# Second token block on the weight operands left from the first, third block's operand sums on VectorE, u sums next to u

## The chip, the cores and the metric

The kernel runs on one core of a Trainium2 chip. The metric is the device time of one execution in microseconds. TensorE (PE) multiplies into PSUM; VectorE (DVE), ScalarE (ACT) and GpSimd (POOL) work on rows of 128 partitions; SyncE (SP) issues the transfers here. Each engine works through its own instructions in order, and semaphores tie the engines together.

## The reference, cut to what matters

Attention over 4 x 8 heads of 576 tokens gives x, 2,304 tokens by 512; then comes a gated feed-forward layer:

```
x = attention(q, k, v, M_prev, z_prev, beta)      # (2304, 512)
g = x @ w_gate                                    # (512, 1536)
silu = g * (1.0 / (1.0 + np.exp(-g)))
val = x @ w_val                                   # (512, 1536)
out = (silu * val) @ w_out                        # (1536, 512)
```

Below, u is silu * val. The change touches the feed-forward layer alone.

## The kernel before, in words

Every product of fp32 numbers is made of three matmuls in fp32r: each operand is split into a high and a low part (a ScalarE cast, a VectorE subtraction), and high x high, high x low and low x high are summed in PSUM.

**Attention** runs over 16 pairs of heads and writes x, in a high and a low part, to the DRAM tensors `xdh` and `xdl`.

**Feed-forward, first product.** The tokens are cut into three blocks of 768 (`ORDER`), the 1,536 features into `NF` = 12 blocks f of 128. A step f takes 128 columns of `w_gate` and of `w_val`. For f = 0 to 2 of block 1 it is a plain product (`eight`). Everywhere else it is a Winograd form of 2 x 2 blocks with seven products instead of eight: `operands(f)` makes the weight side out of the weights `wr[f]` (sums `t`, and high and low parts `th`, `tl`, `bh`, `bl`, two buffers each, which successive f's take in turn), `sums` and the loads of `direct` make the x side (the fourteen tiles `xs` for the block at hand; `x3` for block 3). `chain` gives the seven steps p1, p2, p6, p7, p5, p4, p3, of six matmuls each; step n writes one of two PSUM banks in turn (`ring`), and after most steps ScalarE or VectorE reads that bank. `seven` runs one chain; `plan[n]` holds other work that is issued after step n.

The order on PE, ACT, DVE and POOL is program order (`queued`). The transfers on SP are placed by the scheduler.

- **Block 1, f = 0 to 11.** Its u is split at once, and `lower`, with f one step behind, multiplies it by `w_out`, into six PSUM banks `po`. Beside it the weights of each f arrive in three thirds (`third`), are decoded, kept in DRAM (`wdr`, `wdw`), and the third of `w_out` is split and its two parts stored to `wdo` (in `low_part`). The x side of block 2 is made in f = 6 to 11 (`sums(ORDER[1])`: the loads begin before f = 6, an add of high and low part in plan 5 of each of the next f's).
- **Block 2, f = 0**, alone, with the last `lower` of block 1, and `away`, which takes `po` to the output.
- **Block 3, f = 0**, alone. `sums_on_pool` loads block 3's x from `xdh` and `xdl` and makes its sums and splits on GpSimd.
- **Blocks 2 and 3, f = 1 to 11**, two chains step by step in turn. `stored` makes u (`weighed`) and stores it to `udr`. `tees` makes the four differences of `w_out`'s quarters (`combine` on GpSimd), splits them, and stores both parts to `tdr`.
- **The w_out stage** for blocks 2 and 3: again seven products, in 42 chunks (seven products, two blocks, three chunks `c` of two feature pairs), 18 matmuls of 128x256 in each. `raw_in` loads u's quarters, GpSimd makes one of the sums (six instructions), VectorE the others (`s3`, `s2`, `s4`: 18), `prep` splits a chunk's u, `tee` loads the `w_out` side already split, and `taken` and `out_to` bring the results out.

A double f means one f of blocks 2 and 3 together: 84 matmuls; a single f of one block is 42.

Of the kernel before, what the change touches and what calls it, by code (L numbers as in the profile page):

```python
# [9 lines left out]
F32 = mybir.dt.float32  # L10
# [35 lines left out]
def attention_moe(ctx: ExitStack, tc: tile.TileContext, qt, kt_, v, m, beta, wg, wv, wo, out):  # L46
# [13 lines left out]
    wdo = dram.tile([NF, 128, 2, 512], F32, name="wdo")  # L60
    wdw = dram.tile([NF, 128, 512], F32, name="wdw")
    tdr = dram.tile([4, 2, 128, NF // 2, 256], F32, name="tdr")
    udr = dram.tile([2, 2, 2, 128, NF // 2, N2], F32, name="udr")
# [640 lines left out]
    tmp = tc.alloc_tile_pool(name="tmp", bufs=1, side="right", reuse_waits="tile")  # L704

# [52 lines left out]
    def sums(t0, here=False):  # L758

        got = rot(tmp, "xr", [128, 4, 2, N2], F32, 1)  # L760
        a21, a22, a11, a12 = (got[:, n] for n in range(4))
        s1, s = (rot(tmp, name, [128, 2, N2], F32, 1) for name in ("xt", "xm"))
# [24 lines left out]
    def sums_on_pool(xs, t0, pool_):  # L787

        got = pool_.tile([128, 4, 2, N2], F32, name="xr3")
        s1, s = (pool_.tile([128, 2, N2], F32, name=name) for name in ("xt3", "xm3"))  # L790
        two = (s, s1)
        a21, a22, a11, a12 = (got[:, n] for n in range(4))

        def load(n):
            for dst, src in ((got[:, n], xdh), (two[n % 2], xdl)):
                SP.dma_start(dst, block(src, t0, *AT[n]))  # L796

        load(0)
        load(1)
        for n in range(4):  # L800
            pool.tensor_tensor(got[:, n], got[:, n], two[n % 2], op=ALU.add)
            if n + 2 < 4:
                load(n + 2)
        for p, i, j in (("p1", 0, 0), ("p2", 0, 1), ("p4", 1, 1)):
            direct(xs, t0, p, i, j)

        def parts(p, x):
            h, l = xs[p]
            split_hi(h, x)
            pool.tensor_tensor(l, x, h.bitcast(F32), op=ALU.subtract)  # L810

        pool.tensor_tensor(s1, a21, a22, op=ALU.add)
        pool.tensor_tensor(s, s1, a11, op=ALU.subtract)
        parts("p6", s)
        pool.tensor_tensor(a11, a11, a21, op=ALU.subtract)
        parts("p7", a11)
        parts("p5", s1)
        pool.tensor_tensor(a12, a12, s, op=ALU.subtract)
        parts("p3", a12)

    def high(mix, p, k):
# [29 lines left out]
    def away(j):  # L851
        pt = rot(tmp, "pt", [128, 512], F32, 6)
# [54 lines left out]
    def chain(w, x, bank, use):  # L907
# [28 lines left out]
    def seven(w, x, bank, use, down, plan, away_at):  # L936
        step = chain(w, x, bank, use)
# [10 lines left out]

    def stored(b, f):
# [12 lines left out]
    for f in range(NF):  # L962
        plain, left = f < PLAIN, NF - 1 - f
        plan = [[] for _ in range(4 if plain else 7)]
        if left < 2:
            again(1 - left)
# [3 lines left out]
        if f + 1 >= PLAIN:  # L970
            ready[f + 1], work = operands((f + 1) % NF)
# [68 lines left out]
    tmp.release()  # L1040

    def tees(r, tp):
        w2 = rot(tp, "w2", [128, 2, 512], F32, 2)
        tq = rot(tp, "tq", [128, 4, 256], F32, 1)
        parts = [rot(tp, f"tq{part}", [128, 4, 256], F32R, 2) for part in "hl"]
# [8 lines left out]
        def tops_():  # L1054
            act.copy(parts[0], tq)

        def rest():
            dve.tensor_tensor(parts[1], tq, parts[0].bitcast(F32), op=ALU.subtract)
            for n, x in enumerate(parts):
                SP.dma_start(tdr[:, n, :, r, :].rearrange("i p c -> p i c"), x.bitcast(F32))  # L1060

        return combine, tops_, rest
# [4 lines left out]
    uraw, tset = {}, {}  # L1067
    QUARTER = dict(p1=(0, 0), p2=(0, 1), p6=(0, 0), p7=(1, 0), p4=(1, 0), p5=(1, 1), p3=(0, 1))
    split_in = [xs[p] for p in STEPS] + [x3[p] for p in STEPS]
    ops = {}  # L1070

    def raw_in(p_, b, q, c, of=None):
        if (b, q, c) not in uraw:
            uraw[b, q, c] = p_.tile([128, 2, N2], F32, name=f"u{b}{q[0]}{q[1]}{c}")
        i, j = of or q
        SP.dma_start(uraw[b, q, c], udr[b, i, j, :, 2 * c : 2 * c + 2])

    def prep(n):
        if n >= len(chunks):
            return  # L1080
        k, b, c = chunks[n]
        src = uraw[b, QUARTER[k], c]
        ops[n] = h, l = split_in[n % len(split_in)]
        act.copy(h, src)
        dve.tensor_tensor(l, src, h.bitcast(F32), op=ALU.subtract)
        if k == "p7":
            raw_in(None, b, (1, 0), c, (1, 1))

    wdo_ = wdo.rearrange("(r j) p h c -> j h p r c", j=2)
# [188 lines left out]
```

## Time and profile before

| | us |
|---|---|
| median of 3 runs (lowest to highest) | 642.76 (642.56 to 644.46) |
| the profiled execution | 643.69 |
| its span, first to last instruction | 641.9 |
| busy: PE / DVE / ACT / POOL | 597.7 / 469.9 / 387.5 / 276.9 |
| mean granted TensorE clock over the span | 0.960 |

All rows are from the one profiled execution. Its own time is 1.8 us longer than its span and 0.9 us longer than the median of the runs. The granted clock is 1.00 at 2.4 GHz and 0.50 at 1.2 GHz. A busy TensorE is not one at its peak: its busy time counts slower matmuls at the lower clock as well.

### The profile page before, as it was taken

The numbers are of one execution on the slowest core, as the hardware profiler recorded it, in microseconds if no ns is written. First come the engines' busy times: TensorE is split into PE (matmuls) and PEld (weight loads), VectorE is DVE, ScalarE is ACT, GpSimd is POOL, SyncE is SP. The second block draws the span as 40 slices with busy tenths as digits, with TensorE's granted clock in tenths as the row PEclk, the third lists the DMA queues.
The fourth block names the chain that finished last, engine by engine and source line by source line (L and its number), as shares of the span: only waits on it lengthen the run. The fifth ranks groups of instructions, "written<-read, shape, count | busy, mean of one in ns | idle before, by whom it ended". The sixth has DMA issues, their size and how long they took to land.

```text
span 641.9 us, 11934 instructions
## 1 busy us (share of the span) xinstructions
PE 597.7 (93%) x4118; PEld 549.5 (86%) x4118; DVE 469.9 (73%) x1118; ACT 387.5 (60%) x884; POOL 276.9 (43%) x307
## 2 busy tenths in 40 slices
PE   6999999999999999999972399999999999888997
PEld 4888888878889999999962299999999999778997
DVE  6899999999989888899960045777666556498770
ACT  8889898988876777767550144555555445126711
POOL 6999999999743343344003940223300000530000
PEclk9999999999999999999995589999999999789999
DMA  8366665856276587984759043665559224944642
GB/s 241 124 183 209 198 230 171 261 166 212 91 276 217 189 285 246 383 299 172 253 167 350 16 140 104 204 202 199 180 177 348 82 98 149 383 182 156 238 149 74
DMA packets 69020, 128.45 MB, mean 200 GB/s; under 512 B 8160, under 2 KB 37984, under 8 KB 68960
## 3 DMA queue, kind: packets, MB, share of 16 engines
q1 hardware_dynamic: 68672, 127.41, 59.3%
q8 instruction: 32, 0.52, 0.4%
q10 hardware_dynamic: 288, 0.30, 0.2%
q14 instruction: 28, 0.23, 0.1%
HBM read 82.06 MB, written 45.61 MB: 199 GB/s over the span
## 4 chain that ended last, share of the span: by engine, by line
PE 82%; DMA 6%; POOL 4%; DVE 4%; ACT 2%; issue 1%; SPq 1%; ACTq 0%; POOLq 0%; DVEq 0%
PE s L89 54%; PE tr L89 28%; DMA u<-udr 2%; DVE u L89 2%; DMA xm<-xdl 1%; DMA xr<-xdh 1%; POOL xr L89 1%; DMA qr<-in_qt_dram 1%; DVE yp5l L89 0%; SPq L796 0%; POOL ps L89 0%; DVE oc L89 0%; DMA udr<-zg 0%; DVE yp7l L89 0%; POOL yp3l L89 0%
## 5 line engine op out<-in xcount | busy, mean ns | idle before, releaser
L89 DVE TENSOR_TENSOR zv<-s,zv 128x384 f32<-128x384 f32 x33 | 18.4, 557 | 56.4 <-PE s L89 54.8
L89 POOL TENSOR_SCALAR we<-we 128x512 f32<-128x512 f32 x32 | 25.6, 802 | 74.4 <-ACT we L89 74.3
L89 POOL TENSOR_SCALAR pl<-pl,rs,og 128x384 f32<-128x384 f32 (+1 forms) x64 | 54.0, 855 | 5.0 <-DVE rs L89 4.5
L89 POOL TENSOR_TENSOR u<-u,u 128x768 f32<-128x768 f32 x6 | 14.5, 2438 | 87.4 <-DMA u<-udr 87.3
L89 PE MATMUL tr<-g,vp 128*64 128x320 f32 (+4 forms) x448 | 48.8, 360 | 0.2 <-ACT g L89 0.2
L89 ACT ACTIVATE zh<-zh 128x384 f32<-128x384 f32 x33 | 17.4, 526 | 49.0 <-DVE zh L89 49.0
L89 DVE TENSOR_TENSOR zg<-s,zp 128x384 f32<-128x384 f32 x33 | 18.3, 556 | 38.5 <-PE s L89 21.6
L89 ACT ACTIVATE pl<-pl,mx 128x384 f32<-128x384 f32 (+1 forms) x64 | 42.4, 664 | 4.2 <-DVE mx L89 3.6
L89 PEld LDWEIGHTS tr<-g,vp 128*64 128x64 f32 x448 | 29.3, 137 | 18.1 <-issue 2.3
L89 POOL TENSOR_TENSOR tq<-w 128x256 f32<-128x256 f32 x12 | 10.2, 869 | 71.2 <-DVE tql L89 71.2
L89 PE MATMUL s<-kh,qh 64*128 64x128 f32 (+4 forms) x160 | 36.1, 378 | 4.3 <-POOL qh L89 4.1
L89 ACT COPY zp<-s 128x384 f32<-128x384 f32 x33 | 15.7, 476 | 39.7 <-PE s L89 39.3
L89 DVE CUSTOM_DVE_ANT_0 pl<-s,maskp 128x384 f32<-128x384 f32 (+1 forms) x64 | 38.3, 618 | 0.7 <-PE s L89 0.3
L89 ACT COPY g<-tr 128x384 f32<-128x384 f32 (+1 forms) x60 | 29.9, 524 | 4.7 <-PE tr L89 4.6
L89 POOL TENSOR_SCALAR ps<-ps,rs,og 128x128 f32<-128x128 f32 (+1 forms) x64 | 31.8, 508 | 1.4 <-DVE rs L89 1.4
L89 ACT ACTIVATE ps<-ps,mx 128x128 f32<-128x128 f32 (+1 forms) x64 | 28.6, 454 | 6.1 <-DVE mx L89 6.0
L89 PE MATMUL s<-kl,qh 64*128 64x128 f32 (+4 forms) x160 | 31.1, 325 | 0.9 <-POOL kl L89 0.9
L89 PE MATMUL s<-kh,ql 64*128 64x128 f32 (+4 forms) x160 | 31.1, 325 | 0.0
L89 DVE COPY g<-tr 128x384 f32<-128x384 f32 (+2 forms) x60 | 29.8, 515 | 1.5 <-PE tr L89 1.4
L89 DVE TENSOR_TENSOR tl<-tt,th 128x512 fp32r<-128x512 f32 x42 | 30.5, 727 | 0.0
L89 PE MATMUL tr<-ident,pl 128*128 128x128 f32 x210 | 29.8, 281 | 0.1
L89 DVE TENSOR_TENSOR u<-u,u 128x768 f32<-128x768 f32 x18 | 21.7, 1225 | 10.1 <-POOL u L89 10.1
(483 smaller groups left out, 2332.7 us busy)
## 6 DMA issues: line engine op xcount, KB each, us to landing
u<-udr SPq DMA_DIRECT2D x30, 384.0 KB, 8.6
wraw<-in_wg_dram SPq DMA_DIRECT2D x12, 512.0 KB, 4.4
wraw<-in_wv_dram SPq DMA_DIRECT2D x12, 512.0 KB, 5.1
wraw<-in_wo_dram SPq DMA_DIRECT2D x12, 512.0 KB, 5.0
wr<-wdr SPq DMA_DIRECT2D x12, 512.0 KB, 4.4
qr<-in_qt_dram SPq DMA_DIRECT2D x15, 384.0 KB, 3.1
vp<-in_v_dram SPq DMA_DIRECT2D x16, 320.0 KB, 5.2
xdh<-xh SPq DMA_DIRECT2D x16, 288.0 KB, 4.2
```

The lines of the kernel that those rows point to most:

```text
L89: ins = getattr(eng, name)(*args, **kw)
```

## The change

1. **Order of f.** Block 2 begins with f = 11 and 10 (`LATE`), whose weight operands are still in the two buffers; block 3 follows with f = 10 and 11; then come the double f's, 0 to 9. The operands of f = 0 are made in block 3's f = 11 and no longer in block 1's f = 11.
2. **Block 3's sums.** `sums` takes a pool and a name, and makes block 3's raw sums on VectorE as well: the loads begin at the end of block 1's f = 10 (`begin3`), three adds are in f = 11, the fourth and the four Winograd sums in block 2's f = 11. ScalarE and VectorE split them in block 2's f = 10. `sums_on_pool` goes.
3. **Sums of u.** `mixed` makes the four Winograd sums of u's quarters on VectorE from the tiles in which u was made (128x384), and stores the results; `udr` has a DRAM tensor for each product and block. They run one at a time in the gaps (`some_sums`); the last eight run in the first four chunks of the w_out stage.
4. **w_out in fp32.** `wdo` goes, `tdr` holds unsplit differences, and `split_t` splits the `w_out` side on chip in the w_out stage. Each chunk's u has a load of its own (`load_u`, six ahead), `LEAD` is 3 instead of 5.
5. **Buffers.** `hold` has two buffers of each kind (one of `zv`) in block 1; `pt` has four instead of six; blocks 2 and 3 get their own in the pool `z2`.

```diff
-            if j == 2:
-                for i, o in enumerate((oh, ol)):
-                    SP.dma_start(wdo[f, :, i], o.bitcast(F32))
...
-    def sums(t0, here=False):
-        got = rot(tmp, "xr", [128, 4, 2, N2], F32, 1)
+    def sums(t0, pool_, name, here=False):
+        got = rot(pool_, f"{name}r", [128, 4, 2, N2], F32, 1)
...
-    def sums_on_pool(xs, t0, pool_):
...
-    HOLD = dict(zp=3, zg=4, zh=4, zv=2)
-    hold = lambda name: rot(zwp, name, [128, N2], F32, HOLD[name])
+    hold = lambda name: rot(zwp, name, [128, N2], F32, 1 if name == "zv" else 2)
...
     def stored(b, f):
         def use(i, g, v):
             weighed(g, v)
-            SP.dma_start(udr[b, i, f % 2, :, f // 2], g)
+            kept_u[b, f, i] = g
+            if (f % 2, i) != (0, 1):
+                keep(b, {(0, 0): "p1", (1, 0): "p2", (1, 1): "p4"}[f % 2, i], f, g)
+            if i and (b, f ^ 1, 0) in kept_u:
+                sums_due.extend(mixed(b, f))
         return use
+
+    def mixed(b, f):
+        a11, a21, a12, a22 = (kept_u.pop((b, f // 2 * 2 + j, i)) for j in range(2) for i in range(2))
+        s3, s2 = (rot(z2p, f"zs{n}{b}", [128, N2], F32, 1) for n in range(2))
+        s4 = a11 if f % 2 else a12
+        def one(k, out, x, y, op):
+            def run():
+                dve.tensor_tensor(out, x, y, op=op)
+                keep(b, k, f, out)
+            return run
+        return [
+            one("p7", s3, a11, a21, ALU.subtract), one("p5", a21, a21, a22, ALU.add),
+            one("p6", s2, a22, s3, ALU.subtract), one("p3", s4, a12, s2, ALU.subtract),
+        ]
...
-        if f + 1 >= PLAIN:
-            ready[f + 1], work = operands((f + 1) % NF)
+        if NF > f + 1 >= PLAIN:
+            ready[f + 1], work = operands(f + 1)
...
         if left == 1:
             for k, work in zip((1, 3, 5), due[4:]):
                 plan[k].append(work)
+            begin3, due3, mix3 = sums(ORDER[2], xr3p, "y")
+            plan[6].append(begin3)
         if left == 0:
+            for k, work in zip((0, 1, 5), due3):
+                plan[k].append(work)
...
+    LATE = NF - 1, NF - 2
     plan = [[] for _ in range(7)]
-    again(2)
-    w0 = ready.pop(NF)
-    w1, work = operands(1)
-    for k, some_ in [*enumerate(work), *arrive]:
+    for k, some_ in arrive:
         plan[k] += some_
+    for k, i in ((0, 3), (1, 4), (3, 5), (5, 7), (6, 6)):
+        plan[k].append(due3[i])
-    seven(w0, xs, ring2, stored(0, 0), down, plan, (3, 5, 6))
+    seven(ready[LATE[0]], xs, ring2, stored(0, LATE[0]), down, plan, (3, 5, 6))
...
-    with tc.tile_pool(name="xr3", bufs=1, reuse_waits="tile") as xr3p:
-        sums_on_pool(x3, ORDER[2], xr3p)
-    seven(w0, x3, ring3, stored(1, 0), [], [[] for _ in range(7)], (0, 2, 4))
+    for p, i, j in (("p1", 0, 0), ("p2", 0, 1), ("p4", 1, 1)):
+        direct(x3, ORDER[2], p, i, j)
+    plan = [[] for _ in range(7)]
+    for k, p in ((0, "p6"), (1, "p7"), (2, "p5"), (4, "p3")):
+        plan[k].append(high(mix3, p, both, x3))
+    for k, p in ((1, "p6"), (2, "p7"), (3, "p5"), (6, "p3")):
+        plan[k].append(low(mix3, p, both, x3))
+    seven(ready[LATE[1]], xs, ring2, stored(0, LATE[1]), [], plan, (0, 2, 4), holds(0))
...
+    again(1)
+    w1, work = operands(0)
+    for k in (0, 1, 2, 4):
+        plan[k].append(some_sums)
+    seven(ready[LATE[1]], x3, ring3, stored(1, LATE[1]), [], plan, (0, 2, 4), holds(1))
...
+    plan[0].append(tees(0))
+    seven(ready[LATE[0]], x3, ring3, stored(1, LATE[0]), [], plan, (), holds(1))
...
+    def load_u(n):
+        if n < len(chunks):
+            k, b, c = chunks[n]
+            raw_u[n] = rot(p3a, "ur", [128, 2, N2], F32, U_AHEAD)
+            SP.dma_start(raw_u[n], udr[b, k][:, 2 * c : 2 * c + 2])
...
+    def split_t(n, c):
+        if n < len(KS):
+            k = KS[n]
+            if c == 0:
+                tset[k] = [rot(p3b if n % 2 else p3a, f"t{n % 2}{part}", [128, NF // 2, 256], F32R, 1) for part in "hl"]
+            rows = slice(2 * c, 2 * c + 2)
+            h, l = (x[:, rows] for x in tset[k])
+            act.copy(h, raw_t[k][:, rows])
+            dve.tensor_tensor(l, raw_t[k][:, rows], h.bitcast(F32), op=ALU.subtract)
+            if c == NC - 1:
+                load_t(n + 2)
...
-    for b in range(2):
-        for c in range(NC):
-            s1 = uraw[b, (1, 1), c]
-            pool.tensor_tensor(s1, s1, uraw[b, (1, 0), c], op=ALU.add)
...
-        for s, *which in sums_at.get(n + LEAD, ()):
-            s(*which)
+        at = n // 6
+        if n % 6 in (1, 2, 4):
+            split_t(at + 1, (1, 2, 4).index(n % 6))
+        some_sums(2)
         prep(n + LEAD)
```

In the double f's the plan holds `some_sums` at steps 1, 5, 7 and 9 of 14, `split_t(0, c)` and the first three `prep` in f = 9.

## Rows read from the trace of the kernel before

**Rows 1.** Table by stages (start:end, length, busy us of each engine, granted clock, DMA).
```profile
309.68:321.24 11.56, 11.56 (x61) 10.79 (x61) 10.78 (x22) 7.46 (x17) 0.00 (x0) 1.00 0.86 285
321.24:332.60 11.36, 11.36 (x60) 10.45 (x59) 9.71 (x20) 8.50 (x18) 0.00 (x0) 1.00 0.35 104
332.60:374.65 42.05, 15.47 (x43) 11.91 (x43) 2.25 (x5) 3.99 (x8) 25.89 (x18) 0.55 0.59 204
374.65:535.32 160.67, 160.67 (x925) 160.67 (x925) 101.11 (x188) 80.60 (x161) 19.51 (x23) 1.00 0.50 165
535.32:585.15 49.83, 42.03 (x309) 40.28 (x308) 36.18 (x36) 13.94 (x20) 14.47 (x6) 0.90 0.66 238
585.15:638.49 53.34, 53.33 (x448) 53.12 (x448) 30.82 (x38) 22.11 (x34) 0.00 (x0) 1.00 0.50 171
```
The engines' columns are PE, PEld, DVE, ACT and POOL, with instructions in brackets.

**Rows 2.** Waits of TensorE from 326 to 382 us (total, times, longest).
```profile
PE s L89 <- DMA yp1h<-xdh: 12.6, 1, 12.6
PE s L89 <- POOL yp6h L89: 9.5, 1, 9.5
```

**Rows 3.** Timeline of GpSimd in block 3's f = 0 (start, us).
```profile
355.24 1.80 POOL L89 TENSOR_TENSOR xt<-xr 128x768 f32<-128x768 f32 x1
```

**Rows 4.** Timeline of GpSimd and VectorE at the w_out stage's start.
```profile
553.10 14.58 POOL L89 TENSOR_TENSOR u<-u,u 128x768 f32<-128x768 f32 x6 [87.32 <-DMA u<-udr]
563.40 5.10 DVE L89 TENSOR_TENSOR u<-u,u 128x768 f32<-128x768 f32 x2
```

**Rows 5.** Timeline of VectorE in block 1's f = 11.
```profile
309.75 0.54 DVE L89 SCALAR_TENSOR_TENSOR zg<-s,zg 128x384 f32<-128x384 f32 x1
310.21 0.54 DVE L89 SCALAR_TENSOR_TENSOR zh<-zv,zh 128x384 f32<-128x384 f32 x1
...
311.89 0.56 DVE L89 TENSOR_TENSOR zg<-s,zp 128x384 f32<-128x384 f32 x1
...
314.50 0.95 DVE L89 TENSOR_TENSOR xr<-xr 128x768 f32<-128x768 f32 x1
```

**Rows 6.** Chain that ended last: first and last of eight pieces.
```profile
587.24 6.46 PE tr L89 x54
...
632.00 6.49 PE s L89 x54
```

**Rows 7.** Timeline of TensorE and VectorE at the end of block 2's f = 0.
```profile
331.95 0.39 PE L89 MATMUL tr<-woh,uh 128*128 128x512 f32 x1
...
332.15 0.56 DVE L89 SCALAR_TENSOR_TENSOR zg<-s,zg 128x384 f32<-128x384 f32 x1 [0.54 <-PE s L89]
```

**Rows 8.** Timeline of ScalarE at two places.
```profile
331.95 0.59 ACT L89 ACTIVATE pt<-tr 128x512 f32<-128x512 f32 x1
...
535.18 0.83 ACT L89 CAST xp5h<-u 128x768 fp32r<-128x768 f32 x1
535.91 0.83 ACT L89 CAST xp4h<-u 128x768 fp32r<-128x768 f32 x1
```

**Rows 9.** DMA issues of the whole span (count, KB each, median us to landing).
```profile
u<-udr SPq DMA_DIRECT2D x30, 384.0 KB, 8.6
...
xm<-xdl SPq DMA_DIRECT2D x4, 384.0 KB, 5.4
...
xp1l<-xdl SPq DMA_DIRECT2D x2, 384.0 KB, 3.6
```

**Rows 10.** Timeline of SyncE in block 1's f = 11.
```profile
310.60 0.37 SPq L754 DMA_DIRECT2D xp1l<-xdl  x1
```

**Rows 11.** Table of 2 us slices of the w_out stage, columns as in rows 1.
```profile
548.00:550.00 2.00, 0.32 (x1) 0.11 (x1) 0.00 (x0) 0.87 (x2) 0.00 (x0) 1.00 1.04 375
550.00:552.00 2.00, 1.04 (x5) 1.04 (x6) 0.00 (x0) 0.00 (x0) 0.00 (x0) 0.50 1.03 410
...
556.00:558.00 2.00, 2.00 (x16) 2.00 (x15) 2.00 (x1) 0.00 (x0) 2.00 (x2) 0.80 1.02 393
...
580.00:582.00 2.00, 1.54 (x13) 1.34 (x12) 1.91 (x4) 0.39 (x1) 0.00 (x0) 1.00 0.00 0
```

More of the change, by code (lines that the diff above doesn't have):

```diff
@@ L59, in attention_moe @@
     wdr = dram.tile([NF, 128, 1024], F32, name="wdr")
-    wdo = dram.tile([NF, 128, 2, 512], F32, name="wdo")
     wdw = dram.tile([NF, 128, 512], F32, name="wdw")
-    tdr = dram.tile([4, 2, 128, NF // 2, 256], F32, name="tdr")
-    udr = dram.tile([2, 2, 2, 128, NF // 2, N2], F32, name="udr")
+    tdr = dram.tile([4, 128, NF // 2, 256], F32, name="tdr")
+    udr = {(b, k): dram.tile([128, NF // 2, N2], F32, name=f"u{k}{b}") for k in STEPS for b in range(2)}
     slots = {}
@@ L704, in attention_moe @@
     tmp = tc.alloc_tile_pool(name="tmp", bufs=1, side="right", reuse_waits="tile")
+    xr3p = tc.alloc_tile_pool(name="xr3", bufs=1, side="right", reuse_waits="tile")
     def again(f):
@@ L785, in sums, with high, low @@
         return lambda: (load(0), load(1)), work, mix
-    def sums_on_pool(xs, t0, pool_):
[L789 to L821, printed above, removed]
+    def high(mix, p, k, xs=xs):
         return lambda: act.copy(xs[p][0][:, k], mix[p][:, k])
-    def low(mix, p, k):
+    def low(mix, p, k, xs=xs):
         h, l = xs[p]
@@ L905, in eight, with chain @@
         return u
-    def chain(w, x, bank, use):
+    def chain(w, x, bank, use, hold=hold):
         p1, g1, g2, v2 = hold("zp"), hold("zg"), hold("zh"), hold("zv")
@@ L934, in chain, with seven @@
         return step
-    def seven(w, x, bank, use, down, plan, away_at):
-        step = chain(w, x, bank, use)
+    def seven(w, x, bank, use, down, plan, away_at, hold=hold):
+        step = chain(w, x, bank, use, hold)
         for n in range(7):
@@ L964, in attention_moe @@
         plan = [[] for _ in range(4 if plain else 7)]
-        if left < 2:
-            again(1 - left)
+        if left == 0:
+            again(0)
         for k, i in zip((0, 1, 2) if plain else (2, 4, 6), slots_of[f]):
@@ L980, in attention_moe @@
             if f == 0:
-                _, due, mix = sums(first, True)
+                _, due, mix = sums(first, tmp, "x", True)
                 for k, some_ in enumerate(((0,), (1,), (2, 4), (3,))):
@@ L995, in attention_moe @@
             if left == 5:
-                begin, due, mix = sums(ORDER[1])
+                begin, due, mix = sums(ORDER[1], tmp, "x")
                 begin()
@@ L1017, in attention_moe @@
             u = [None, None]
-            seven(ready.pop(f), xs, ring2, lambda i, g, v: weigh(u, i, g, v), down, plan, ())
+            seven(ready[f], xs, ring2, lambda i, g, v: weigh(u, i, g, v), down, plan, ())
         before = (f, u)
@@ L1052, in combine @@
                 pool.tensor_tensor(tq[:, n], a, b, op=ALU.subtract)
[L1054 to L1062, printed above, removed]
+            SP.dma_start(tdr[:, :, r, :].rearrange("i p c -> p i c"), tq)
+        return combine
+    plan = [[] for _ in range(7)]
+    for k, some_ in enumerate(work):
+        plan[k] += some_
+    plan[0].append(tees(0))
+    seven(ready[LATE[0]], x3, ring3, stored(1, LATE[0]), [], plan, (), holds(1))
     NC = 3
@@ L1078, in prep @@
-    def prep(n):
[L1079 to L1089, printed above, removed]
+    ops, raw_u, raw_t, tset = {}, {}, {}, {}
+    U_AHEAD, LEAD = 6, 3
+    def load_u(n):
[3 more added lines that the diff above has]
+            SP.dma_start(raw_u[n], udr[b, k][:, 2 * c : 2 * c + 2])
@@ L1103, in attention_moe @@
     p3a = None
-    T_AT = range(2, 8)
-    for f in range(1, NF):
+    T_AT = range(0, 5)
+    for f in range(NF - 2):
         plan = [[] for _ in range(14)]
-        again(f + 2)
+        if f + 2 < NF - 2:
+            again(f + 2)
         w, w1 = w1, None
-        if f + 1 < NF:
+        for k in (1, 5, 7, 9):
+            plan[k].append(some_sums)
+        if f + 1 < NF - 2:
             w1, work = operands(f + 1)
@@ L1112, in attention_moe @@
                 plan[2 * k] += some_
-        if f == 1:
-            tp = tc.alloc_tile_pool(name="tp", bufs=1, side="right", reuse_waits="tile")
         if f in T_AT:
-            for k, work in zip((1, 7, 11), tees(f - T_AT[0], tp)):
-                plan[k].append(work)
+            plan[1].append(tees(1 + f))
         if f == T_AT[-1] + 1:
@@ L1226, in attention_moe @@
     p3a.release()
+    z2p.release()
     x3p.release()
```

103 lines of the change are left out of this document (47 added, 56 removed).

## The prediction

> **What bounds the kernel now.** I read the table by stages first. From 309.68 to 332.60 us, from 374.65 to 535.32 us and after 585.15 us TensorE is busy without a gap at a granted clock of 1.00; two stretches are not like that: 332.60 to 374.65 (15.47 us busy of 42.05, clock 0.55) and 535.32 to 585.15 (42.03 of 49.83, clock 0.90) [rows 1]. So an edit pays where it fills these two stretches, and costs where it makes a gap in the others.
>
> The first stretch is block 3's first feature block, alone. The waits of TensorE name its cause: 12.6 us for the load of yp1h, 9.5 us for GpSimd's yp6h [rows 2]. GpSimd makes the four raw sums, the Winograd sums and the splits of block 3 there, at 1.80 us a sum; it is busy 25.89 us of the 42.05 [rows 1, 3], and everything is behind the loads of `xdh` and `xdl`, which start only when block 2's first feature block has ended.
>
> The second stretch is the start of the w_out stage. The u sums on GpSimd take 14.58 us for six, and two of VectorE's beside them 5.10 us [rows 4], where a sum of that size takes VectorE 0.95 us in block 1 [rows 5]. Behind it, eight pieces of the chain hold 54 matmuls each; the first starts at 587.24, the last ends at 638.49: 51.25 us for 432, 0.1186 us a matmul [rows 6].
>
> **Part 1: block 3's sums move to VectorE, blocks 2 and 3 begin on operands of f = 11 and 10.** The matmuls are the same 84 for each f and both blocks. Before: one f with block 1's `lower` beside it (11.36 us), one alone (42.05 us), eleven double ones, 160.67 / 11 = 14.61 us each [rows 1]. After: the same 11.36 us, three single ones, ten double ones. A single one is half a double one, 7.30 us. Two of the three are the double one that goes; the third stands against 42.05 us: **-34.75 us**, less what is lost in the singles and in getting the sums ready.
>
> *The singles.* With one chain and two banks, step n+2 writes the bank that step n's reader must have left; between lies one step, 7.30 / 7 = 1.04 us. A reader starts 0.20 us after the step's last matmul has issued (the next matmul starts at 331.95, VectorE's read at 332.15) and takes 0.56 us [rows 7]: 0.28 us is spare. In the trace instructions follow each other 0.08 to 0.10 us sooner than their durations say (309.75 to 310.21 on VectorE, 535.18 to 535.91 on ScalarE, 0.73 for 0.83) [rows 5, 8]; I walked the two queues with that. In block 2's f = 10 ScalarE has, besides the chain, four casts of 0.73 us and three `away` of 0.49 [rows 8]. Counted from that f's first matmul: copy of p1 1.24 to 1.63, cast of p6 to 2.36, `away` to 2.85, then silu of g1 (VectorE's sum ends at 2.84) to 3.3, cast of p7 to 4.05, and only then the copy of g2, ready at 3.32, which ends at 4.55: step 4, due at 4.16, waits 0.4 us. Cast of p5 and `away` follow, so the copy of v2 begins at 5.65 and ends at 6.15: step 5, due at 5.6, waits 0.55. That is 1.0 us in sum. Block 3's f = 10 has only four sums of 128x384, 0.46 us each [rows 5], in VectorE's gaps: 0. Block 3's f = 11 has `operands(0)`: ScalarE's cast of 512 columns (two thirds of 0.73) delays the copy of g2 by 0.35 us, and GpSimd's four `combine` slow VectorE there, 0.5 us: 0.9 us. I take **+1.9 us**; between 0.5 (the casts of plan 0 done early) and 6 (each of 21 steps 0.28 us late).
>
> The operands of f = 10 and 11 lie in the two slots of `tt`'s splits, and `operands(0)` writes only after f = 10's last read, so no reload is on the path. Block 3's direct loads may start when block 1's last `lower` has read; block 2's f = 10 covers them for 8.3 us, and a load of 384 KB lands in 3.6 to 5.4 us [rows 9]: nothing, or, without the cover, what the rival below says.
>
> *The new wait.* `begin3` issues the first loads of `xdh` and `xdl` behind the last VectorE instruction of f = 10 (ends 310.21 + 0.54 = 310.75 [rows 5]), and the first add is put on VectorE in step 0 of f = 11, right after the `halves`. VectorE is in order: behind the add stand g1's sum (now at 311.89 [rows 5]), which frees the bank of step 1, and everything after. With some 0.5 us of queue for the second load and 3.6 us to land, as for xp1l in the same place [rows 9, 10], the data is there at about 314.9. The add takes 0.95, g1's sum 0.56: 316.4. Step 3 is due at 314.2 (f = 11 begins at 309.68 and lasts 11.56 us [rows 1]; steps of 1.04, all but the first with 0.69 of `lower` behind them), so it waits 2.2 us. VectorE then works off its queue without a further wait, because f = 11 loses 2,816 columns of `operands`, 3.2 us at 0.87 per 768, for three adds of 0.87. Idle time of 1.68 and 0.96 us in the two slices from 548 to 552 was followed by a granted clock of 0.50, still below 1.00 in the slice from 556 [rows 11]; some 6 us at half speed lose about 3.2 us. The gap here is a little shorter, so I take half of that, 1.6: **+3.8 us** in all. Ends: 2.2 (no fall) and 9.0 (block 2's direct loads, issued from 310.60 on [rows 10], go ahead: the second load issued at 313.0, 5.4 us as for xm [rows 9], 5.8 us of gap, and the whole fall).
>
> In block 2's f = 11 five 768-wide sums (4.35 us) take the place of `operands(1)` (3.2 us); VectorE was busy 9.71 of 11.36 us there [rows 1], so 10.9: covered by TensorE's 11.36, the last sum slips by 1.2 us into f = 10 and is needed at its plan 4. Nothing.
>
> **Part 2: sums of u in the double f's.** 40 sums of 128x384 in the ten f's, four per f, 1.8 us; the split of w_out's differences (1024 wide) goes. VectorE is busy 101.11 of 160.67 us now [rows 1], 9.2 of 14.61 per f, so 11.0 after, and a bank has three other steps' time to be left. The stores of u go from four to seven per f, 192 KB each, on a DMA share of 0.50 [rows 1]. Nothing; if the cover went, each sum would cost its 0.46 us, 18 us.
>
> **Part 3: the w_out stage.** Out go 24 stores of `wdo` in block 1, six GpSimd sums and VectorE's 18; eight 128x384 sums stay, done in the first four chunks; new are 21 casts and subtractions of 128x512. VectorE per chunk, by columns: 0.87 for the low part, 0.58 for a split in one chunk of two, 0.13 for outputs (three products of seven, once in three chunks), in the first four 0.93 of sums: up to 2.4 us, against 18 x 0.1186 = 2.13 us of TensorE and three chunks of lead. It keeps ahead. Loads: 42 of 384 KB in place of 30, w_out 768 KB seven times in place of fourteen; in bytes, 22 MB against 23. So 42 chunks take 42 x 2.13 = 89.7 us instead of 49.83 + 53.34 = 103.17 [rows 1]: -13.5; with 0.5 for the start **-13.0 us**, and between -13.5 and -8.5 (two waits of 2.6 us, the idle time of the slices from 548 to 552 [rows 11]).
>
> The 24 stores less and the fewer buffers of `hold` cost or give nothing in block 1: TensorE is busy all the time in its f = 11 [rows 1], where both would be felt too, and each buffer's reader is done a whole f before it is written again.
>
> **Sum**, against the profiled execution's 643.69 us (span 641.9 and 1.8 around it): 643.7 - 34.75 + 1.9 + 3.8 - 13.0 = 601.7. The median of the runs lies 0.9 us under that execution, so **601 us**.
>
> **The clock, weighed.** After gaps of 0.46 us (580 to 582, TensorE 1.54 of 2.00 us) the granted clock stays at 1.00 [rows 11]; so the small waits of the singles should leave it at the upper level, 2.4 GHz. The Trainium skill (TensorE: Matmul & The Clock Gate, "A second HAM failure mode: psum-queue depth-cycling") says that an engine that goes round its PSUM banks and idles a little between groups again and again can move between the two levels. By that rule the singles would run at the lower level, and the sum would be 22 us more; the row speaks against it, though for chunks of eighteen matmuls, not of six.
>
> **The rivals.**
> - *Direct loads first.* SP sends block 2's xp1 and xp2 before block 3's raw loads; the upper end of the new wait. For it: they are ready at 310.60, 0.15 us before [rows 5, 10]. Against: the raw loads come earlier in the program. 601 + 5 = 606.
> - *Block 3's operands late all the same.* If `yp1h` lands 12.6 us after block 1's last `lower`, as now [rows 2], block 2's f = 10 hides 8.3, and 4.3 and a fall of the clock stay: 608. Against: six raw loads that stood ahead of it in the queue are gone.
> - *The singles at the lower clock.* 126 matmuls at twice 0.174 us: 623.
> - *The w_out stage waits for its loads, in part.* Each chunk now needs a load of its own, six deep; a u load takes 8.6 us now [rows 9], 8.6 / 6 = 1.4 us per chunk. If SP's order holds some back behind output stores and only four fly, 2.15 us, on the edge; with 0.3 us more in each chunk, 613.
> - *Slower than before.* The same place: the gain of 42 us is gone when a chunk takes 2.13 + 42 / 42 = 3.1 us, that is when fewer than 2.8 loads of 8.6 us are in flight. With two it is 4.3 us a chunk, 601 + 91 = 692. Against: after 585.15 us TensorE does not wait, with loads of u and w_out in that stretch too [rows 1].
>
> **Chances.** Forecast (595 to 605) 0.66; direct loads first 0.12; operands late 0.06; lower clock 0.05; loads in part 0.09; slower 0.02. The range takes in the first three and most of the partly late loads, down to a new wait of nothing and singles without loss (595) and up to 612. All cases but the last are more than 0.3% faster, which is about what a measurement of this kernel can tell from no change; 0.01 for an end within it.
>
> **What would show it.** Right: no stretch of TensorE under 9 tenths between blocks; GpSimd without sums there; the double f's at 14.6 us and ten of them; the w_out stage in about 90 us at clock 1.00; one wait of TensorE on VectorE's g1 sum in f = 11 of 2 to 3 us, behind a VectorE wait for the load of the new raw tile. Wrong: waits for yp1h or for u loads of several us, a clock of 0.50 in the singles, VectorE behind in the double f's.

## The result, and the profile after

| | before | after |
|---|---|---|
| median, us (lowest to highest, runs) | 643.09 (642.56 to 644.46, 4) | 604.75 (604.64 to 605.62, 4) |
| the profiled execution, us | 643.69 | 605.62 |
| its span, us | 641.9 | 603.7 |
| mean granted TensorE clock | 0.960 | 0.992 |

The ratio is 0.9404, with an interval of 0.9386 to 0.9421: faster, inside the range of 595 to 612, 3.75 us above the 601 that was predicted.

The page of the changed kernel, its part on busy times and two of its rows of forty slices:

```profile
span 603.7 us, 11980 instructions
...
PE 587.5 (97%) x4118; PEld 542.7 (90%) x4118; DVE 482.6 (80%) x1161; ACT 392.0 (65%) x895; POOL 240.1 (40%) x285
...
PE   5999999999999999999998999999999999999997
...
PEclk9899999999999999999998999999999999999999
```

TensorE was busy 597.7 us before and is busy 587.5 us now: 10 of the 38 us are busy time, of matmuls that ran slowly, the other 28 are gaps. After the start one slice is left that shows an 8 on both rows, the 22nd; it begins at 316.9 us, in block 1's f = 11.

The table by stages of the changed kernel answers to [rows 1], with the same columns. In order: block 1's f = 11, block 2's f = 11 (with the last `lower`), block 2's f = 10, block 3's f = 10, block 3's f = 11, the ten double f's, the w_out stage.

```profile
311.06:328.12 17.06, 13.40 (x62) 12.11 (x60) 10.13 (x18) 5.43 (x12) 0.00 (x0) 0.90 0.96 331
328.12:339.68 11.56, 11.56 (x62) 10.79 (x60) 9.91 (x19) 6.49 (x14) 0.00 (x0) 1.00 0.20 71
339.68:348.11 8.43, 7.88 (x44) 7.23 (x43) 5.76 (x9) 6.41 (x12) 0.00 (x0) 1.00 0.99 321
348.11:355.46 7.35, 7.35 (x44) 7.23 (x44) 5.29 (x10) 2.38 (x6) 0.00 (x0) 1.00 1.02 353
355.46:364.97 9.51, 7.87 (x43) 7.22 (x43) 8.15 (x12) 4.41 (x10) 7.54 (x9) 1.00 0.70 229
364.97:511.06 146.09, 146.09 (x842) 146.09 (x842) 104.19 (x203) 68.46 (x143) 14.57 (x16) 1.00 0.52 177
511.06:600.35 89.29, 89.14 (x757) 88.74 (x756) 59.51 (x83) 47.32 (x73) 0.00 (x0) 1.00 0.73 250
```

The stretch of 42.05 us at a clock of 0.55 is gone, and so is the gap at the start of the w_out stage. Two stages are longer than their matmuls: f = 11 (17.06 us, 13.40 busy, clock 0.90) and the third single (9.51 us, 7.87 busy). What TensorE waited for between 290 and 370 us (total, times, longest):

```profile
PE s L88 <- DVE zg L88: 3.7, 1, 3.7
PE s L88 <- DVE zvw L88: 1.1, 1, 1.1
PE s L88 <- ACT zh L88: 0.8, 2, 0.6
PE s L88 <- ACT zvw L88: 0.3, 1, 0.3
```

The two long waits of [rows 2], 12.6 us for yp1h and 9.5 us for yp6h, are gone; a wait of 3.7 us for VectorE's g1 sum is new. The prediction's terms beside what the stages give, each as a difference to the kernel before. The stages of the changed kernel begin at an f's first matmul. In [rows 1] the first two begin 0.16 us behind it: the first matmul of block 1's f = 11 is at 309.52 us there and that of block 2's first f at 321.08, so that the second lasts 11.52 us and not 11.36. The table goes by the first matmuls.

| us | predicted | measured | how measured |
|---|---|---|---|
| up to f = 11 | 0 | +1.5 | its first matmul: 309.52 to 311.06 |
| f = 11 of block 1 | +3.8 | +5.5 | 11.56 to 17.06 |
| block 2's first f | 0 | 0.0 | 11.52 to 11.56, from its first matmul |
| lone f and one double become three singles | -34.75 + 1.9 = -32.85 | -31.4 | 42.05 + 14.61 to 8.43 + 7.35 + 9.51 = 25.29 |
| ten double f's | 0 | 0.0 | 146.06 to 146.09 |
| w_out stage | -13.0 | -13.9 | 103.17 to 89.29 |
| sum | -42.05 | -38.2 | spans: 641.9 to 603.7 |

The 1.5 us ahead of f = 11 do not show a cost of the change: in the five experiments below that have the same code up to this place (2, 5, 6, 7 and 8) f = 11 begins between 309.60 and 310.11 us. They are there before the feed-forward layer begins, whose first matmul is at 185.22 us and was at 183.66. From 15 to 30 us, in the attention, the granted clock is 0.83 in this execution and was 0.92, with TensorE busy throughout: 0.09 of 15 us is 1.35 us. Why the clock was lower there in this execution stays open; experiment 6 has 1.00 in the same stretch.

**The new wait**, in the trace. VectorE's timeline in f = 11 (start, us, then the idle time before and its releaser):

```profile
312.88 0.55 DVE L88 TENSOR_TENSOR ul<-zh,uh 128x384 fp32r<-128x384 f32 x1
317.95 0.96 DVE L88 TENSOR_TENSOR yr<-yr,ym 128x768 f32<-128x768 f32 x1 [4.52 <-DMA ym<-xdl]
318.83 0.55 DVE L88 TENSOR_TENSOR zg<-s,zp 128x384 f32<-128x384 f32 x1
```

TensorE's timeline at the same place:

```profile
319.44 0.46 PE L88 MATMUL s<-xp7h,th 128*128 128x384 f32 x1 [3.66 <-DVE zg L88]
```

SyncE's timeline, the issues of the loads:

```profile
312.14 0.37 SPq L751 DMA_DIRECT2D xp1l<-xdl  x1
312.61 0.41 SPq L765 DMA_DIRECT2D yr<-xdh  x1
313.08 0.46 SPq L765 DMA_DIRECT2D ym<-xdl  x1
...
314.61 0.52 SPq L751 DMA_DIRECT2D xp1h<-xdh  x1
315.54 0.36 SPq L751 DMA_DIRECT2D xp2h<-xdh  x1
```

The chain that ended last goes through that load, with its time to landing:

```profile
313.08 4.79 DMA ym<-xdl
```

Read from the bottom up: SP sends one direct load of block 2, then the raw loads, then the other direct ones; `ym` lands 4.79 us after 313.08; VectorE's add stands for 4.52 us, and behind it stands the sum `zg` that frees the bank TensorE needs. Everything here is the wait that the prediction describes, and longer. VectorE then stands once more, 1.32 us for the second add's load (`yt`, to 320.70), where the prediction has no further wait; the list above shows no wait of TensorE for it. Then the clock, in slices of 2 us (columns as above):

```profile
316.00:318.00 2.00, 0.00 (x0) 0.00 (x0) 0.04 (x1) 0.00 (x0) 0.00 (x0) 1.00 0.94 319
318.00:320.00 2.00, 0.56 (x3) 0.57 (x4) 1.38 (x2) 0.58 (x2) 0.00 (x0) 1.00 1.03 364
320.00:322.00 2.00, 2.00 (x9) 1.71 (x8) 1.30 (x2) 0.31 (x1) 0.00 (x0) 0.65 1.06 386
322.00:324.00 2.00, 2.00 (x8) 2.00 (x7) 1.74 (x3) 1.70 (x4) 0.00 (x0) 0.50 1.07 378
324.00:326.00 2.00, 2.00 (x12) 1.82 (x11) 1.62 (x4) 0.95 (x3) 0.00 (x0) 0.99 1.07 373
...
344.00:346.00 2.00, 1.45 (x8) 1.08 (x7) 1.85 (x3) 2.00 (x5) 0.00 (x0) 1.00 1.01 360
```

The gap of 3.66 us is followed by 0.65, 0.50 and 0.99. Over the stage the clock is 0.90, so 0.10 of 17.06 = 1.7 us are lost to it: 3.66 + 1.7 = 5.4 of the 5.5 us. The last line is from block 2's f = 10, with two gaps of some 0.3 us in 2 us: the clock stays at 1.00, the upper level, 2.4 GHz.

### The profile page after: what moved, and what is told of

The parts are those of the page before. It is cut to its first block, busy times and chain, and to the rows that moved or that the text cites. A ratio compares the mean times of both kernels' runs of the same rounds, so it can differ in the third digit from the quotient of the medians.

```text
span 603.7 us, 11980 instructions
## 1 busy us (share of the span) xinstructions
PE 587.5 (97%) x4118; PEld 542.7 (90%) x4118; DVE 482.6 (80%) x1161; ACT 392.0 (65%) x895; POOL 240.1 (40%) x285
## 4 chain that ended last, share of the span: by engine, by line
PE 89%; DVE 4%; DMA 2%; ACT 2%; issue 1%; POOL 1%; SPq 0%; DVEq 0%
PE s L88 58%; PE tr L88 31%; DMA kr<-in_kt_dram 1%; DMA ym<-xdl 1%; DVE tt L88 1%; DMA up<-zh 1%; DVE zg L88 1%; DVE xr L88 0%; DVE bl L88 0%; DVE zh L88 0%; DVE tl L88 0%; POOL ps L88 0%; ACT g L88 0%; ACT we L88 0%; POOL kl L88 0%
## 5 line engine op out<-in xcount | busy, mean ns | idle before, releaser
L88 ACT ACTIVATE zg<-zg 128x384 f32<-128x384 f32 x33 | 17.3, 524 | 25.0 <-DVE zg L88 24.5
L88 PEld LDWEIGHTS tr<-ident,pl 128*128 128x128 f32 x210 | 23.4, 143 | 6.5 <-issue 3.5
L88 DVE TENSOR_TENSOR tl<-tt,th 128x512 fp32r<-128x512 f32 x38 | 28.0, 737 | 0.0
L88 ACT CAST th<-tt 128x512 fp32r<-128x512 f32 x38 | 23.7, 623 | 6.6 <-DVE tt L88 5.5
L88 DVE TENSOR_TENSOR zvw<-s,zvw 128x384 f32<-128x384 f32 x23 | 12.7, 556 | 18.5 <-PE s L88 17.2
L88 PEld LDWEIGHTS s<-kh,qh 64*128 64x128 f32 (+1 forms) x160 | 19.1, 195 | 8.5 <-POOL qh L88 4.1
```

Source lines behind the costliest of these rows:

```text
L88: ins = getattr(eng, name)(*args, **kw)
```

## The experiments

All ratios are to the kernel before, run on the same chip; the change's own is 0.9404. Diffs are against the changed kernel.

**1. The raw loads one f earlier (`e1_loads_earlier`).** Is the new wait a matter of when the load starts?

```diff
         if left == 2:
+            begin3, due3, mix3 = sums(ORDER[2], xr3p, "y")
+            plan[6].append(begin3)
...
         if left == 1:
-            begin3, due3, mix3 = sums(ORDER[2], xr3p, "y")
-            plan[6].append(begin3)
```

> The changed kernel with one move: the first loads of block 3's raw x (begin3) are issued in step 6 of block 1's f = 9 instead of f = 10, one f (11.6 us) earlier; the adds stay where they are. Theory (VectorE's in-order queue stands behind the first add, which waits 4.5 us for ym; TensorE then waits 3.7 us for g1's sum and runs some 4 us at the lower clock): both go, f = 11 takes 11.6 us instead of 17, time 599.4 (598.8 to 600.5). Rival (the DMA traffic of 14 loads in f = 11, or VectorE's own work there, is what is late): f = 11 stays above 14 us and the time stays above 602.

Measured: 599.70 us, ratio 0.9323 (0.9307 to 0.9339). By stages, f = 11 and block 2's first f:

```profile
309.94:321.48 11.54, 11.54 (x62) 10.77 (x61) 8.56 (x15) 5.51 (x12) 0.00 (x0) 1.00 0.88 285
321.48:334.50 13.02, 12.09 (x61) 10.64 (x60) 11.27 (x20) 6.29 (x14) 0.00 (x0) 1.00 0.34 123
```

f = 11 is back at 11.54 us and a clock of 1.00. The wait has not gone altogether; VectorE's timeline shows the first and the third add:

```profile
312.21 0.95 DVE L88 TENSOR_TENSOR yr<-yr,ym 128x768 f32<-128x768 f32 x1
...
322.07 0.96 DVE L88 TENSOR_TENSOR yr<-yr,ym 128x768 f32<-128x768 f32 x1 [2.28 <-DMA ym<-xdl]
```

The third add now stands 2.28 us for its load, which SP sends behind block 2's direct loads, and block 2's first f takes 13.02 us, 1.46 more than in the changed kernel. The cause of the long wait is shown: the load's start, and nothing in the add.

**2. GpSimd in VectorE's place, with the early start (`e2_gpsimd_early`).** Was it the engine or the start that made block 3's sums late before?

```diff
-    def sums(t0, pool_, name, here=False):
+    def sums(t0, pool_, name, here=False, dve=dve):
...
-            begin3, due3, mix3 = sums(ORDER[2], xr3p, "y")
+            begin3, due3, mix3 = sums(ORDER[2], xr3p, "y", dve=pool)
...
-    for k, p in ((0, "p6"), (1, "p7"), (2, "p5"), (4, "p3")):
-        plan[k].append(high(mix3, p, both, x3))
-    for k, p in ((1, "p6"), (2, "p7"), (3, "p5"), (6, "p3")):
-        plan[k].append(low(mix3, p, both, x3))
+    for p in ("p6", "p7", "p5", "p3"):
+        split_hi(x3[p][0], mix3[p])
+        pool.tensor_tensor(x3[p][1], mix3[p], x3[p][0].bitcast(F32), op=ALU.subtract)
```

> The changed kernel with block 3's eight sums and four splits on GpSimd again, begun at the same place as now (loads at the end of f = 10), the splits after block 1's last lower. Theory (what cost 34 us was that this work began only when nothing else was left to do, not the engine): GpSimd needs some 25 us, is done before block 3 asks for each part, VectorE's queue has no wait in it, ScalarE no casts in block 2's f = 10: 598.5 (597.5 to 601). Rival (GpSimd's 1.80 us a sum against VectorE's 0.95 is what cost): block 3's first f waits for yp6, yp7, yp5 and yp3 as before, 5 us or more: above 606.

Measured: 603.29 us, ratio 0.9379 (0.9365 to 0.9394), so as fast as the change, 4.8 us above the expectation. The waits of TensorE from 309 to 364 us, three of the eight:

```profile
PE s L88 <- DMA xp1h<-xdh: 1.7, 1, 1.7
...
PE s L88 <- POOL yp5l L88: 0.8, 1, 0.8
...
PE s L88 <- POOL yp3l L88: 0.7, 1, 0.7
```

GpSimd makes TensorE wait 1.5 us, where it was 9.5 for yp6h alone [rows 2]. So the earlier start, with block 2's f = 11 and 10 as its cover, made nearly all of the difference, and not the engine. The engine is still worth something: block 3's f = 10 takes 10.22 us here and 7.35 in the changed kernel. GpSimd with the loads one f earlier, as VectorE has them in experiment 1, was not run, nor was VectorE with the start of before. The expectation missed two things. SP sends block 2's xp1h at 315.20 us, behind six raw loads where the changed kernel has four before it, and TensorE waits 1.7 us for it. And GpSimd slows VectorE; VectorE's timeline in block 3's first f:

```profile
344.52 2.08 DVE L88 TENSOR_TENSOR zs<-zg,zh 128x384 f32<-128x384 f32 x1
...
347.62 2.20 DVE L88 TENSOR_TENSOR zs<-zh,zs 128x384 f32<-128x384 f32 x1
350.70 0.56 DVE L88 TENSOR_TENSOR zvw<-s,zvw 128x384 f32<-128x384 f32 x1 [0.88 <-PE s L88]
```

GpSimd's timeline beside them:

```profile
344.11 2.08 POOL L88 TENSOR_TENSOR yp7l<-yr,yp7h 128x768 fp32r<-128x768 f32 x1
...
347.37 2.03 POOL L88 TENSOR_TENSOR yp5l<-yt,yp5h 128x768 fp32r<-128x768 f32 x1
...
350.60 1.85 POOL L88 TENSOR_TENSOR yp3l<-yr,yp3h 128x768 fp32r<-128x768 f32 x1
```

Two sums of 128x384 take 2.08 and 2.20 us beside GpSimd's subtractions, 0.55 each in the changed kernel without them, while the one that reads `s` in PSUM takes 0.56 us beside the third. The Trainium skill (GPSIMD Engine Reference, "1. Specifications") says that GpSimd shares its SBUF interfaces with VectorE and contends with VectorE instructions that have two SBUF inputs; these rows agree.

**3. Weights of f = 0 and 1 loaded again instead of the operands left on chip (`e4_weights_again`).**

```diff
-    LATE = NF - 1, NF - 2
+    LATE = 0, 1
+    again(2)
+    ready[0] = ready.pop(NF)
+    ready[1], work = operands(1)
...
-    for k, some_ in arrive:
+    for k, some_ in [*enumerate(work), *arrive]:
...
-        if NF > f + 1 >= PLAIN:
-            ready[f + 1], work = operands(f + 1)
+        if f + 1 >= PLAIN:
+            ready[f + 1], work = operands((f + 1) % NF)
```

The reloads (`again`) move with it, and the double f's become 2 to 11.

> The changed kernel with the order of f of the kernel before: blocks 2 and 3 begin with f = 0 and 1, whose operands are made anew from DRAM in block 1's f = 11 and block 2's f = 0, beside the new sums; then f = 2 to 11 double. Theory (the operands left on chip are worth what VectorE's 3.3 us per f cost where its queue is already late): f = 11, with 3.3 us more behind a 4.5 us wait, gets 2 to 4 us longer, block 2's first f, with 14 us of VectorE work in 11.4, about 2 us: 609 (606 to 611). Rival (the reload is hidden, the operands on chip are worth nothing): 604.8 within 0.8.

Measured: 607.23 us (605.73 to 608.73), ratio 0.943 (0.941 to 0.9449). The median is 2.5 us above the change's, on another chip, and the two intervals overlap from 0.9410 to 0.9421: it is slower by little, if at all, but inside the expected range. The place is not the one expected: f = 11 takes 17.80 us, 0.7 more, and TensorE's wait behind the load there is longer by as much (4.4 us for 3.7), so the extra weight sums, which stand behind the add, show no cost of their own. Block 2's first f shows one:

```profile
328.28:341.69 13.41, 12.57 (x62) 10.46 (x60) 13.41 (x26) 7.82 (x18) 0.00 (x0) 1.00 0.30 93
```

VectorE is busy for all of its 13.41 us, against 9.91 of 11.56 in the changed kernel. What the operands on chip are worth is mostly VectorE's room beside block 3's sums, 1.85 us in that stage; the three singles take 26.17 us, 0.9 more.

**4. The first half alone (`e5_first_part_alone`).** The order of f and block 3's sums as changed; u's sums, `wdo` and `tdr` in two parts, and the w_out stage as before.

```diff
-    tdr = dram.tile([4, 128, NF // 2, 256], F32, name="tdr")
+    wdo = dram.tile([NF, 128, 2, 512], F32, name="wdo")
+    tdr = dram.tile([4, 2, 128, NF // 2, 256], F32, name="tdr")
+    udr = dram.tile([2, 2, 2, 128, NF // 2, N2], F32, name="udr")
...
-            if i and (b, f ^ 1, 0) in kept_u:
-                sums_due.extend(mixed(b, f))
+            SP.dma_start(udr[b, i, f % 2, :, f // 2], g)
```

> The changed kernel with its first half alone: order of f and block 3's sums on VectorE as changed, but u sums, w_out parts (wdo, tdr), loads and the w_out stage as in the kernel before. Theory (the two halves are independent; the first brings 34.6 less 5.5 in f = 11 and 3.4 in the singles): 643.1 - 25.8 = 617.3 (615 to 620), the w_out stage 103 us long with its waits. Rival (the w_out stage's waits came from what stood before it, and go with it): below 610.

Measured: 617.47 us, ratio 0.9599 (0.9575 to 0.9623). So the first half gives 4.0 of the 6.0 per cent, the second the rest. f = 11 takes 18.09 us here, the three singles 23.55, the w_out stage 103.75 against 103.17 in [rows 1]: the first half does nothing for that stage, and keeps its own gain without the second.

**5. The differences of w_out one f later (`e10_combine_later`).** The third single takes 9.51 us where 8.2 were predicted. Is it GpSimd's `combine`?

```diff
-    plan[0].append(tees(0))
...
-    T_AT = range(0, 5)
+    T_AT = range(0, 6)
...
-            plan[1].append(tees(1 + f))
+            plan[1].append(tees(f))
```

> The changed kernel with w_out's first differences (combine, four GpSimd subtractions of 128x256) moved out of block 3's single f = 11 into the double f's, where the other five are (one in each of f = 0 to 5). Theory (block 3's f = 11 takes 9.5 us instead of 7.35 because GpSimd's subtractions slow VectorE's operand work for f = 0; in the run of the first part alone, without them there, it took 7.8): 7.9 us, time 603.1 (602.7 to 603.6). Rival (operands(0) and its casts alone make it long): 604.8 within 0.5.

Measured: 604.76 us, ratio 0.9391 (0.9377 to 0.9406): no gain, and the rival's figure. GpSimd's timeline in that single, after the edit:

```profile
358.18 2.10 POOL L88 TENSOR_TENSOR tq<-w,tq 128x256 f32<-128x256 f32 x2
360.24 2.32 POOL L88 TENSOR_TENSOR tq<-w 128x256 f32<-128x256 f32 x2
```

The subtractions are still there. GpSimd has nothing else to do, and nothing but their loads holds them, so a later place in the program does not make them run later. The edit had not tested the cause.

**6. The same, held back by its loads (`e11_combine_held`).** As in 5, and the loads of `combine` wait for the VectorE instruction that stands last at that place.

```diff
-        for j in range(2):
-            SP.dma_start(w2[:, j], wdw[2 * r + j])
...
+            for j in range(2):
+                ld = SP.dma_start(w2[:, j], wdw[2 * r + j])
+                follow(ld, last[DVE], "not before this step", mybir.DependencyClass.Sync)
```

> The run with combine in the double f's, with one addition: the loads of w_out's rows that combine reads wait for VectorE's last instruction of that step, so that GpSimd, which has nothing else to do, can't run ahead. (In the run without this GpSimd had eight subtractions between 356.8 and 366 all the same, and VectorE's 128x512 instructions beside them took 1.2 us instead of 0.68.) Theory (these slow VectorE in block 3's f = 11): that f takes 7.9 us instead of 9.5, time 603.2 (602.6 to 603.8). Rival (the casts and sums of operands(0) make it long): 604.8 within 0.6, f = 11 above 9 us.

Measured: 602.58 us, ratio 0.9365 (0.9347 to 0.9383). The third single by stages, with GpSimd idle:

```profile
354.67:362.52 7.85, 7.59 (x43) 7.27 (x43) 5.89 (x12) 4.37 (x10) 0.00 (x0) 1.00 0.14 50
```

The same experiment's timeline of VectorE, one instruction of that single:

```profile
359.15 0.68 DVE L88 TENSOR_TENSOR tl<-tt,th 128x512 fp32r<-128x512 f32 x1
```

The timeline of the changed kernel has the same instruction beside GpSimd's:

```profile
361.20 1.22 DVE L88 TENSOR_TENSOR tl<-tt,th 128x512 fp32r<-128x512 f32 x1
```

0.68 against 1.22 us, and the single 7.85 against 9.51. 1.7 us of the third single are GpSimd's subtractions, by way of VectorE: this run shows it, where 5 could not.

**7. The sums of u on GpSimd (`e6_u_sums_on_gpsimd`).**

```diff
-                dve.tensor_tensor(out, x, y, op=op)
+                pool.tensor_tensor(out, x, y, op=op)
```

> The changed kernel with the 48 sums of u's quarters (128x384) on GpSimd instead of VectorE, at the same places. Theory (in the double f's either engine has room, so the place of the sums matters and not the engine): the double f's stay at 14.6 us, time 604.8 (604 to 606.5; the four sums in block 3's f = 10 and the eight at the start of the w_out stage may cost up to 1.5 us). Rival (what made the w_out stage short is that GpSimd no longer slows VectorE): double f's of 15 us or more, or waits in the w_out stage: above 608.

Measured: 606.70 us, ratio 0.9427 (0.9413 to 0.944), 0.2 above the range expected. The ten double f's do not feel it:

```profile
364.08:510.16 146.08, 146.08 (x841) 146.08 (x841) 102.78 (x167) 67.78 (x143) 54.78 (x52) 1.00 0.53 178
```

146.08 us, as with VectorE: there is cover for the sums on either engine. The loss is in the w_out stage, 91.60 us against 89.29, which holds the last eight sums, and 0.5 us in the third single (9.99). At that stage's start VectorE's splits of 128x768 take 1.77 us beside GpSimd's sums and 0.95 behind them, and TensorE waits for three of them, 1.8 us in all: there the rival's cause is at work. The interval overlaps the change's own from 0.9413 to 0.9421.

**8. Two loads of u in flight instead of six (`e3_two_loads_ahead`).** The rival on the slower side rests on this.

```diff
-    U_AHEAD, LEAD = 6, 3
+    U_AHEAD, LEAD = 2, 3
```

> The changed kernel with two u loads in flight in the w_out stage instead of six. Theory (the stage is short because its loads are far enough ahead; a load of 4 to 5 us, the cast and the low part of 1.8 us, two at a time, give 3.1 us a chunk against TensorE's 2.13): the stage takes about 130 us instead of 89, time 640 (625 to 655), which uses up nearly all that the change gains. Rival (loads land so fast that two are enough): below 612.

Measured: 629.96 us (two runs), ratio 0.9787 (0.9769 to 0.9805). The w_out stage by stages:

```profile
510.18:624.20 114.02, 99.92 (x757) 91.56 (x756) 61.49 (x83) 48.62 (x73) 0.00 (x0) 1.00 0.67 209
```

The same experiment's DMA issues, the loads of u (count, KB each, median us to landing):

```profile
ur<-up SPq DMA_DIRECT2D x42, 384.0 KB, 3.4
```

The same row of the changed kernel's page:

```profile
ur<-up SPq DMA_DIRECT2D x42, 384.0 KB, 4.8
```

114.02 us for 42 chunks are 2.71 us each, against the 3.1 expected and 2.13 with six in flight: the stage goes by its loads, as the prediction's rival said, but with 3.4 us to landing and not the 8.6 of [rows 9]. By the expectation's own sum, 3.4 us and the split's 1.8 for two chunks at a time are 2.6 us a chunk.

**9. What is left of the waits, moved (`e9_best`).** Experiment 1, the third add moved from step 5 of f = 11 to step 1 of block 2's first f, the fourth there from step 0 to step 2, and the edit of 5.

```diff
-            for k, work in zip((0, 1, 5), due3):
+            for k, work in zip((0, 1), due3):
...
-    for k, i in ((0, 3), (1, 4), (3, 5), (5, 7), (6, 6)):
+    for k, i in ((1, 2), (2, 3), (2, 4), (3, 5), (5, 7), (6, 6)):
```

> The changed kernel with three moves: block 3's first loads one f earlier (as in the run above that did this alone), its third add moved from block 1's f = 11 to step 1 of block 2's first f and the fourth add to step 2 there (in that run the third add waited 2.3 us for its load and block 2's first f took 13.0 us instead of 11.6), and w_out's first differences in the double f's. Theory: f = 11 11.6 us, block 2's first f 11.6, singles 8.4, 7.35 and 7.9: 599.7 - 1.45 - 1.6 = 596.7 (596 to 598). Rival (the waits only move to the next consumer of the loads): 598.5 or more.

Measured: 598.59 us, ratio 0.9304 (0.929 to 0.9318). f = 11 and block 2's first f take 11.56 us each, as expected; the third single takes 9.75 for 7.9, since `combine` had not moved (5). So the time is above the range and at the rival's figure, but the waits have not moved to other consumers of the loads.

**10. All of it (`e12_all_moves`).** Experiment 9 with the loads of `combine` held as in 6, and `away` of block 2's f = 10 moved to block 3's f = 10.

```diff
-    seven(ready[LATE[1]], xs, ring2, stored(0, LATE[1]), [], plan, (0, 2, 4), holds(0))
+    seven(ready[LATE[1]], xs, ring2, stored(0, LATE[1]), [], plan, (), holds(0))
```

> The best run so far (loads one f earlier, third and fourth add one f later) with combine held in the double f's and the last three away moved from block 2's f = 10 to block 3's f = 10, where ScalarE has no casts. Theory: block 3's f = 11 7.9 us instead of 9.7, block 2's f = 10 7.9 instead of 8.4: 598.6 - 2.3 = 596.3 (595.5 to 597.2). Rival (GpSimd's subtractions, now later, make VectorE late in the double f's): double f's above 14.7 us, 598 or more.

Measured: 596.77 us (596.28 to 597.19), ratio 0.9274 (0.926 to 0.9289), 8 us faster than the change. By stages, from f = 11 to the third single:

```profile
309.63:321.19 11.56, 11.56 (x61) 10.79 (x60) 9.05 (x17) 5.52 (x12) 0.00 (x0) 1.00 0.90 293
321.19:332.75 11.56, 11.56 (x61) 10.79 (x60) 10.93 (x20) 6.48 (x14) 0.00 (x0) 1.00 0.49 165
332.75:340.76 8.01, 7.75 (x44) 7.22 (x42) 5.77 (x9) 5.00 (x9) 0.00 (x0) 1.00 0.98 324
340.76:348.12 7.36, 7.36 (x44) 7.24 (x43) 5.29 (x10) 3.80 (x9) 0.00 (x0) 1.00 0.69 251
348.12:355.97 7.85, 7.59 (x44) 7.28 (x43) 5.88 (x12) 4.35 (x10) 0.00 (x0) 1.00 0.15 54
```

The five stages take 46.34 us, against 53.91 in the changed kernel. The only wait of TensorE that the list still shows between 305 and 360 us is for ScalarE, 0.5 us in two parts.

## Why the prediction was right, point by point

- **Block 3's lone f.** -34.75 held: ten double f's at 14.61 us, three singles, no wait for yp1h. Experiment 2 adds that the early start of the loads, with block 2's two f's as cover, does nearly all of this; the move to VectorE, which gives Part 1 its name, is the smaller part.
- **The singles, +1.9.** Mis-sized, 25.29 against 23.8. The first was walked to 8.3 and took 8.43, the second 7.3 and took 7.35. The failing term is the third, "GpSimd's four `combine` slow VectorE there, 0.5 us": it took 9.51 against 8.2. GpSimd does the next four subtractions as well in that stretch, nine instructions by the table, and VectorE's 128x512 splits lose half a us each beside them (experiments 5 and 6).
- **The new wait, +3.8.** The mechanism was right, with its place, releaser and queue; the size was 5.5. The step that was too small is "3.6 us to land": the load took 4.79 us, with a DMA share near 1 from 314 us on. Counted from the first matmul of f = 11, the data was there after 317.87 - 311.06 = 6.8 us, where 314.9 - 309.52 = 5.4 were predicted; 1.2 of the 1.4 us are the landing, the rest is that SP sent it a little later, behind xp1l. This gives the gap of 3.66 for 2.2. The fall of the clock, taken as 1.6, was 1.7. The rival *direct loads first* came true in one load of four: xp1l went ahead of the raw loads, xp1h and the two of xp2 behind them.
- **The w_out stage, -13.0.** -13.9. Its 89.29 us lie 0.4 under 42 x 18 matmuls of 0.1186 us, 89.7; the 0.5 for the start was not lost.
- **The parts costed at nothing.** The sums of u: 146.09 us for ten double f's; experiment 7 shows the cover is there on GpSimd too. The operands left on chip: no reload on the path; loading again costs 2.5 us in the medians, whose intervals overlap (experiment 3).
- **Rivals.** *Operands late*: no. *Lower clock*: the singles ran at 1.00, with two gaps of 0.3 us in the first (the slice from 344), and of 0.6 and 1.1 us in the third. The Trainium skill, as the prediction weighed it (TensorE: Matmul & The Clock Gate, "A second HAM failure mode: psum-queue depth-cycling"), says that small idle times between groups of matmuls, often enough, can move the clock between its levels; this trace shows no such move at these gaps. *Loads in part* and *slower*: no, 42 loads landed in 4.8 us with six in flight. The price of the second was too high: two in flight were to give 692 us, and experiment 8 measured 629.96. The prediction took the 8.6 us of before as fixed, and the landing time falls as fewer are in flight.
- **The rest of the miss.** 605.62 less 601.65 is 4.0 us: 1.5 ahead of f = 11, 1.7 in the new wait, 1.5 in the singles, less 0.9 in the w_out stage; 0.2 are rounding and the ends of the span. The first 1.5 us are mostly the clock of this execution in the attention, which no term of the prediction covers.

## What to carry to other kernels

An in-order engine that is given an instruction waiting for a load passes the wait on to everything behind it: start the load at least a stage earlier, and look at which loads stand in front of it in the queue, also for the later pieces. When work moves off a slow engine and starts earlier at the same time, ask which of the two pays; here it was nearly all the start. To make an idle engine work later, something must hold it; a later place in the program does nothing.

## What the runs showed of the hardware that was not expected

- VectorE beside GpSimd: 128x512 with two inputs in SBUF 0.68 us alone, 1.22 us beside 128x256 subtractions; 128x384 0.55 us alone and 2.08 to 2.20 us beside 128x768 ones, while an instruction that reads PSUM stayed at 0.56 us.
- The granted clock answers late: after a gap of 3.66 us that ended at 319.44 it is still 1.00 in the slice to 320, 0.65 and 0.50 in the next two, when TensorE is busy again, and 0.99 in the one from 324.
- A load of 384 KB landed in 3.4 us (median) with two in flight and in 4.8 us with six.
